# Attention's product with v in a piece for each block of tokens, at a rate of 0.75

## The chip, the core and the metric

The program runs on one core of one Trainium2 chip. A core has five engines that run side by side, each with its own instruction stream: TensorE (PE, with PEld for its weight loads), VectorE (DVE), ScalarE (ACT), GpSimd (POOL) and SyncE (SP, which here only issues DMA). Every engine takes its instructions in order; one that waits holds up all that stand behind it. The metric is the device time of one execution in microseconds (us), and lower is better.

## What is computed

Three stages follow one another, all in float32. Attention runs over 8 batches with 8 heads, 576 tokens and a head width of 64; keys and values are first averaged in groups of 8 tokens, so that each token looks at 72 of them.

```python
k_p = k.reshape(B, H, Sp, pool, D).mean(axis=3)
v_p = v.reshape(B, H, Sp, pool, D).mean(axis=3)
scores = scale * np.matmul(q, k_p.transpose(0, 1, 3, 2))
attn = softmax(scores)
x = np.matmul(attn, v_p)          # then as 4608 tokens x 512
h = (x @ w1) * (x @ w2) @ w3 @ w_out
r = np.maximum(h @ w_in, 0.0)
out = (r * r) @ w_out2
```

The inner widths are 1024 for w1, w2 and w3, and 2048 for the last stage.

## The kernel before

**Arithmetic.** A float32 operand is held as two parts, high and low, in a format that TensorE takes in one pass (fp32r); `mm3` makes each product of three matmuls (high by high, high by low, low by high). `split` writes such a pair: a copy on ACT for the high part, a subtraction on DVE for the low one.

**Stages.** `fold` first multiplies w3 by w_out into one matrix, W. Then come nine blocks of 512 tokens. Block i runs `stage_ab(i, u)` for u from 0 to 7 (a = x @ w1, b = x @ w2 for 128 of the 1024 columns, and gf = a * b on DVE), and two steps behind it `stage_w(i, u)`, which adds that piece times W into four accumulators. In the profile the matmuls of the blocks are `ps_w<-x,wt` (the first half of w1 and w2, held in SBUF), `ps_w<-x,un` (the second half, read back from DRAM through a ring of 8 buffers) and `acc<-gt,Wt`. After the last block comes the third stage (`ps_a` to `ps_d`, `ps_h`, `o`), which holds nothing of attention.

**Attention** makes x, and is spread through `fold` and the blocks. `build_tasks` writes one list of tasks: transposed keys (`pe_kt`), scores (`pe_s`), transposed probabilities (`pe_t`), and the product with v (`pe_av`, tile `ps_av`). A batch has two halves, of 256 and 320 tokens; `pe_av` is called for each of them with four pairs of heads (hp), and makes 128 of x's 512 rows, in one tile of PSUM from the pool of two that all attention tasks share. Three matmuls come from `mm3` and one holds the rest (`rem`). The result is copied into the x tiles of the blocks that the tokens fall in. Seven halves lie in two blocks: in batch 0 (256 tokens and 64), batch 1 (192 and 128), batch 2 (128 and 192), batch 3 (64 and 256), all in the second half, and in the first half of batch 5 (192 and 64), batch 6 (128 and 128) and batch 7 (64 and 192).

**What sets the order.** `run_mm` calls `tick` after each 6 matmuls. A tick runs the pumps: `attend`, which adds `rate[0]` to a credit and writes tasks from the head of the list while the credit is at least 1, and feeders that prepare the weights of the third stage (`feed_quarters`). A task has a list `need`; when it is not in `done`, the list stands still. The x tiles are a pool of 8, which is two blocks of four, so a task that writes block n must wait until `("ab", n - 2)` is done, that is until the `stage_ab` steps of block n - 2 are all written. For a half that lies in two blocks, `need` goes by the later one. Before block i, `until(lambda: tokens_ready((i + 1) * TB))` ticks with no matmul between until all the halves that block i needs have been written. It does so 2, 9, 5, 4, 5 and 4 times ahead of blocks 1, 2, 3, 5, 6 and 7, and not ahead of the others. A scheduler afterwards moves instructions within small bounds on each engine.

**DMA.** SP issues all loads in order. `load_v(b + 1)`, called after batch b's last `pe_av`, issues 24 and more; `load_q` 16 of queries, which DVE transposes (`qT<-qraw`). Raw weights (`raw`, `rq`) are loaded there too, and ACT takes each up first (L136).

Of the kernel before, what the change touches and what calls it, by code (L numbers as in the profile page):

```python
# [8 lines left out]
F32 = mybir.dt.float32  # L9
# [6 lines left out]
P = 128  # L16
TB = 512
# [12 lines left out]
def attn_moe_moe2_kernel(  # L30
# [16 lines left out]
    nc = tc.nc  # L47
# [16 lines left out]
    QT = []  # L64
# [43 lines left out]
    def f32(ap):  # L108
        return ap.bitcast(F32)
# [45 lines left out]
    def mm3(ps, pairs, first=True, last=True):  # L155

        todo = []
        for (ah, al), (bh, bl) in pairs:
            todo += [(ah, bh), (ah, bl), (al, bh)]
        n = len(todo)  # L160
        return [
            (lambda a=a, b=b, i=i: nc.tensor.matmul(  # L162
                ps, a, b, start=first and i == 0, stop=last and i == n - 1))
            for i, (a, b) in enumerate(todo)
        ]
# [63 lines left out]
    def xt_tile(blk, c):  # L229
        if (blk, c) not in xt:  # L230
            xt[blk, c] = x_p.tile([P, 2, TB], F32R, tag="x", name=f"x_{blk}_{c}")
        return xt[blk, c]
# [164 lines left out]
        dl = rem[RB:2 * RB, :, c0:c0 + n]  # L397
        nc.vector.tensor_sub(dl, ps[RB:2 * RB, :2, :n], f32(dl))

    def pe_av(b, hf, hp):  # L400
        hi, lo, rem = atts[b, hf]
        s0 = QT[HALF[hf][0]][0]
        w = sum(QT[i][1] for i in HALF[hf])
        ps = ps_at.tile([P, TB], F32, tag="at", name="ps_av")
        st = [vl[:, i, hp].rearrange("p a d -> p (a d)") for i in range(2)]
        for m in mm3(ps[:, :w], [(st, [t[:, hp, :w] for t in (hi, lo)])], last=False):
            m()
        nc.tensor.matmul(
            ps[:, :w], vr[:, hp].rearrange("p a d -> p (a d)"), rem[:, hp // 2, :w],
            start=False, stop=True)  # L410
        t0 = b * S + s0
        pieces = []
        o = 0
        while o < w:
            blk, c = divmod(t0 + o, TB)
            n = min(w - o, TB - c)
            pieces.append((blk, c, o, n))
            o += n

        for blk, c, o, n in pieces:  # L420
            nc.scalar.copy(xt_tile(blk, hp)[:, 0, c:c + n], ps[:, o:o + n])
        for blk, c, o, n in pieces:
            t = xt_tile(blk, hp)
            nc.vector.tensor_sub(t[:, 1, c:c + n], ps[:, o:o + n], f32(t[:, 0, c:c + n]))  # L424
        done.add(("av", b, hf, hp))

    NG = B * len(QT)

    def s_end(hf):
        return QT[HALF[hf][-1]][0] + QT[HALF[hf][-1]][1]  # L430

    def build_tasks():


        order = []
        pend = []

        def put(fn, need=()):
            order.append((need, fn))

        def put_pend(n=1):
            for _ in range(min(n, len(pend))):
                order.append(pend.pop(0))

        def kt(b):
            for part in range(2):
                put(lambda part=part: pe_kt(b, part))

        def sc(g):
            for half in range(2):  # L450
                put(lambda half=half: pe_s(g, half))
                put_pend()

        kt(0)
        sc(0)
        put(lambda: load_q(0, 1))
        for g in range(NG):
            b, i = divmod(g, len(QT))
            hf = 0 if i in HALF[0] else 1

            if i + 1 == HALF[1][0] and b + 1 < B:
                put(lambda b=b: load_q(b + 1, 0))
            if i + 1 == len(QT) and b + 1 < B:
                put(lambda b=b: load_q(b + 1, 1))
                kt(b + 1)
            if g + 1 < NG:
                sc(g + 1)
            if i == HALF[hf][0]:
                put_pend(len(pend))
            for part in range(2):  # L470
                put(lambda g=g, part=part: pe_t(g, part))
                put_pend()
            if i == HALF[hf][-1]:
                need = [("v", b)]

                last = (b * S + s_end(hf) - 1) // TB
                if last >= 2:
                    need.append(("ab", last - 2))
                for hp in range(NP):
                    def av(b=b, hf=hf, hp=hp):  # L480
                        pe_av(b, hf, hp)
                        if hf == 1 and hp == NP - 1 and b + 1 < B:
                            load_v(b + 1)
                    pend.append((need, av))
                if b < EARLY:
                    put_pend(len(pend))
        put_pend(len(pend))
        return order
# [17 lines left out]

    def tokens_ready(n):

        b, s = divmod(n, S)
        halves = [(bb, h) for bb in range(b) for h in range(2)]  # L510
        if s:
            halves.append((b, 0))
            if s > QT[HALF[1][0]][0]:
                halves.append((b, 1))
        return all(("av", bb, h, hp) in done for bb, h in halves for hp in range(NP))


    wt = {}
# [523 lines left out]
    setup_consts()  # L1042
    fold()
    until(lambda: tokens_ready(TB))
    rate[0] = 0.6
    fh1 = [(nm_, w, kc) for nm_, w in (("w1", w1), ("w2", w2)) for kc in range(KD)]
    feeds = []
    second = []
# [151 lines left out]
```

## Time and profile before

| | us |
|---|---|
| runs | 1644.57, 1641.16, 1642.05 |
| median | 1642.05 |
| profiled execution | 1644.58 |
| its span in the trace | 1642.8 |
| `fold`, from the start of the trace | 0 to 136 |
| block 0 | 136 to 240 |
| blocks 1 to 8 | 240 to 907 |
| third stage | 907 to 1643 |

The blocks begin at 135.9, 240.3, 325.2, 413.8, 502.3, 582.3, 666.3, 755.1 and 834.0 us. A time in a row is the start within the span; the number in brackets is what the engine stood idle before it, and whom it waited for. Records of matmuls overlap, so the spacing of starts tells what one costs. `PEclk` is the share of TensorE's full clock that was granted.

### The profile page before, as it was taken

To read this page: it belongs to the slowest core of one execution; us is meant where nothing else is said; L and a number is where in the kernel's file an instruction comes from. 1 tells how busy PE (TensorE), PEld (TensorE's weight loads), DVE (VectorE), ACT (ScalarE), POOL (GpSimd) and SP (SyncE) were. 2 spreads that over 40 slices of the span, in tenths; PEclk is the share of its full clock that TensorE was granted. 3 is DMA by queue.
4 is the path that set the end of the run, shared out by engine and by line. 5 is a ranking of instruction groups with operands and counts; after the bars stand their busy time and mean duration, and the time that the engine had idled before them with its cause. 6 is when DMAs were issued, how large, how long until landed. Compare 5 with 4: busy or idle time off the path is not lost.

```text
span 1642.8 us, 24999 instructions
## 1 busy us (share of the span) xinstructions
PE 1561.0 (95%) x8480; PEld 1309.5 (80%) x8480; DVE 1024.7 (62%) x1842; ACT 749.8 (46%) x1833; POOL 148.9 (9%) x194
## 2 busy tenths in 40 slices
PE   7899789999998999999999999999999999999998
PEld 5556567777777778777887788899899899899998
DVE  8898757565856457575626548547864776476432
ACT  4454425444443234445323566456444645454441
POOL 1132302111111011111101000000000000000000
PEclk9999799999999999999999999999999999999999
DMA  8454575747466554565726877677767777776764
GB/s 260 146 156 128 161 212 141 206 131 204 132 171 183 161 164 153 169 174 178 262 84 199 281 193 221 188 213 203 238 188 212 211 206 195 206 213 186 210 209 153
DMA packets 277854, 308.26 MB, mean 188 GB/s; under 512 B 98272, under 2 KB 163808, under 8 KB 277728
## 3 DMA queue, kind: packets, MB, share of 16 engines
q1 hardware_dynamic: 272544, 297.23, 61.6%
q10 hardware_dynamic: 5184, 9.44, 1.6%
q8 instruction: 68, 1.11, 0.3%
q14 instruction: 58, 0.48, 0.1%
HBM read 247.46 MB, written 56.62 MB: 185 GB/s over the span
## 4 chain that ended last, share of the span: by engine, by line
PE 66%; DVE 10%; DMA 7%; issue 3%; ACT 2%; SPq 2%; POOL 2%; DVEq 0%; POOLq 0%; ACTq 0%
PE o L964 17%; PE ps_w L162 16%; PE acc L162 7%; PE ps_a L876 5%; PE ps_c L876 5%; PE ps_d L876 5%; PE ps_h L162 3%; PE o L1020 3%; PE ps_b L876 2%; DMA rq<-in_moe_w_in_dram 2%; DVE x2o L114 1%; PE ps_s L343 1%; DMA raw<-in_moe_w_out_dram 1%; DMA un<-u_w 1%; SPq L276 1%
## 5 line engine op out<-in xcount | busy, mean ns | idle before, releaser
L964 PEld LDWEIGHTS o<-un,gt 128*128 128x128 f32 x2688 | 342.5, 191 | 19.3 <-DVE gt L114 7.3
L964 PE MATMUL o<-un,gt 128*128 128x256 f32 x2688 | 347.2, 283 | 6.1 <-DVE gt L114 5.7
L114 DVE TENSOR_TENSOR gt<-gs,gt 128x512 fp32r<-128x512 f32 x221 | 151.8, 690 | 198.7 <-ACT gt L113 198.4
L162 PE MATMUL ps_w<-x,wt 128*128 128x512 f32 x864 | 231.9, 411 | 9.5 <-DVE x L424 4.6
L162 PE MATMUL ps_w<-x,un 128*128 128x512 f32 x864 | 221.1, 403 | 11.0 <-DMA un<-u_w 9.4
L162 PE MATMUL acc<-gt,Wt 128*128 128x512 f32 x864 | 218.0, 396 | 4.2 <-ACT st L650 2.8
L113 ACT CAST gt<-gs 128x512 fp32r<-128x512 f32 x221 | 135.9, 616 | 158.5 <-PE o L964 128.0
L162 PEld LDWEIGHTS ps_w<-x,un 128*128 128x128 f32 x864 | 162.0, 192 | 46.4 <-DMA un<-u_w 11.5
L162 PEld LDWEIGHTS ps_w<-x,wt 128*128 128x128 f32 x864 | 161.4, 195 | 46.2 <-DVE x L424 7.0
L162 PEld LDWEIGHTS acc<-gt,Wt 128*128 128x128 f32 x864 | 158.8, 188 | 38.7 <-ACT st L650 3.8
L360 ACT ACTIVATE att<-ps_s,mx 128x72 f32<-128x72 f32 (+1 forms) x320 | 98.1, 320 | 103.8 <-DVE mx L358 97.7
L883 ACT ACTIVATE r<-r 128x512 f32<-128x512 f32 x96 | 60.6, 632 | 122.1 <-DVE r L913 121.7
L876 PE MATMUL ps_a<-x2o,un 128*128 128x512 f32 x384 | 99.6, 395 | 2.1 <-ACT p L901 2.1
L876 PE MATMUL ps_c<-x2o,un 128*128 128x512 f32 x384 | 99.5, 395 | 0.0
L876 PE MATMUL ps_d<-x2o,un 128*128 128x512 f32 x384 | 98.5, 391 | 0.0
L624 DVE TENSOR_TENSOR gf<-asb,ps_w 128x512 f32<-128x512 f32 x72 | 49.2, 684 | 71.0 <-PE ps_w L162 68.7
L884 ACT ACTIVATE gs<-r 128x512 f32<-128x512 f32 x137 | 85.4, 630 | 3.4 <-ACT gt L113 0.5
L876 PEld LDWEIGHTS ps_c<-x2o,un 128*128 128x128 f32 x384 | 70.6, 191 | 13.4 <-DVE u L907 0.3
L876 PEld LDWEIGHTS ps_a<-x2o,un 128*128 128x128 f32 x384 | 69.3, 190 | 14.7 <-ACT p L901 2.5
L876 PEld LDWEIGHTS ps_d<-x2o,un 128*128 128x128 f32 x384 | 69.8, 189 | 12.9
L620 ACT COPY asb<-ps_w 128x512 f32<-128x512 f32 x72 | 42.3, 588 | 81.2 <-PE ps_w L162 80.9
L113 ACT CAST gt<-gf 128x512 fp32r<-128x512 f32 x72 | 44.8, 623 | 74.2 <-DVE gf L624 65.6
(123 smaller groups left out, 2133.2 us busy)
## 6 DMA issues: line engine op xcount, KB each, us to landing
un<-u_w SPq DMA_DIRECT2D x144, 256.0 KB
un<-u_A SPq DMA_DIRECT2D x128, 256.0 KB
un<-u_S SPq DMA_DIRECT2D x128, 256.0 KB
un<-u_oA SPq DMA_DIRECT2D x128, 256.0 KB
un<-u_oS SPq DMA_DIRECT2D x128, 256.0 KB
raw<-in_moe_w_dram SPq DMA_DIRECT2D x32, 512.0 KB
raw<-in_moe_w_out_dram SPq DMA_DIRECT2D x24, 512.0 KB
x2d<-st ACTq DMA_DIRECT2D x36, 256.0 KB
```

Source lines behind the costliest of these rows:

```text
L113: nc.scalar.copy(hi, src)
L114: (eng or nc.vector).tensor_sub(lo, src, f32(hi))
L162: (lambda a=a, b=b, i=i: nc.tensor.matmul(ps, a, b, start=first and i == 0, stop=last and i == n - 1))
L276: nc.sync.dma_start(f32(vr)[r0:r0 + RM, c, 1, :], vhl[c * RM:(c + 1) * RM, i // 2, NP, :])
L360: nc.scalar.activation(av[:, h0 + h], sv[:, h], ACTF.Exp, bias=mx[:n, h:h + 1], scale=scale, accum_out=sm[:n, h0 + h:h0 + h + 1])
L620: nc.scalar.copy(asb, ps)
L624: nc.vector.tensor_mul(gf, asb, pss[1])
L876: nc.tensor.matmul(ps, l, r, start=first and j == 0, stop=j == len(todo) - 1, skip_group_check=True)
L883: nc.scalar.activation(t, src, ACTF.Relu)
L884: nc.scalar.activation(take(name), t, ACTF.Square)
L964: nc.tensor.matmul(ps, l, r, start=u == 0 and m != 5 and o % 2 == 0 and j == 0, stop=u == NU - 1 and j == 2, skip_group_check=True)
L1020: nc.tensor.matmul(acc[o][:, y * PC:(y + 1) * PC], l, r, start=u == 0 and y == 0 and j == 0, stop=u == U2 - 1 and j == 2, skip_group_check ...
```

## The change

`pe_av` makes the product for one piece only, the part of a half that falls in one block. `av_pieces` lists the pieces. In `build_tasks` each piece is a task of its own for each hp, and its `need` names its own block; `tokens_ready` asks for the pieces that lie before token n, and no longer for whole halves. The rate goes from 0.6 to 0.75. `split` writes the two parts, as the two loops did.

```diff
-    def pe_av(b, hf, hp):
+    def av_pieces(b, hf):
         s0 = QT[HALF[hf][0]][0]
         w = sum(QT[i][1] for i in HALF[hf])
-        for m in mm3(ps[:, :w], [(st, [t[:, hp, :w] for t in (hi, lo)])], last=False):
...
+    def pe_av(b, hf, hp, piece):
+        hi, lo, rem = atts[b, hf]
+        blk, c, o, n = piece
+        for m in mm3(ps[:, :n], [(st, [t[:, hp, o:o + n] for t in (hi, lo)])], last=False):
+            m()
+        nc.tensor.matmul(
+            ps[:, :n], vr[:, hp].rearrange("p a d -> p (a d)"), rem[:, hp // 2, o:o + n],
+            start=False, stop=True)
+        t = xt_tile(blk, hp)
+        split(t[:, 0, c:c + n], t[:, 1, c:c + n], ps[:, :n])
+        done.add(("av", b, hf, hp, blk))
...
-                last = (b * S + s_end(hf) - 1) // TB
-                if last >= 2:
-                    need.append(("ab", last - 2))
+                for piece in pieces:
+                    need = [("v", b)]
+                    if piece[0] >= 2:
+                        need.append(("ab", piece[0] - 2))
...
-    rate[0] = 0.6
+    rate[0] = 0.75
```

The list grows from 255 tasks to 283, by 28 `pe_av` calls. They bring 112 matmuls and 112 weight loads; ACT and DVE keep their number of instructions for x. The ticks without matmuls ahead of the blocks are gone, at all nine. `load_v(1)`, which stood just ahead of block 0, now stands within it. `feed_quarters` is some seven steps further back in its list at the ends of the middle blocks.

How TensorE's instructions stand at the start of block 6. The block's first matmuls are `ps_w...<-x_0_...,wt`; a number behind a name tells tiles of one name apart, and `x_0` to `x_3` are the four tiles of a block. Before:

```order
L162 MATMUL acc_5812<-gt,Wt 128x512 x3
L162 MATMUL ps_av<-aT_6107,vl 128x256
L162 MATMUL ps_av<-aT_6108,vl 128x256
L162 MATMUL ps_av<-aT_6107,vl 128x256
L408 MATMUL ps_av<-aR,vr 128x256
L343 MATMUL ps_s<-kbd,qT 128x144 x2
L162 MATMUL ps_w_6415<-x_0_5488,wt 128x512
```

And now:

```order
L162 MATMUL ps_av<-aT_6124,vl 128x128
L162 MATMUL ps_av<-aT_6125,vl 128x128
L162 MATMUL ps_av<-aT_6124,vl 128x128
L420 MATMUL ps_av<-aR,vr 128x128
L162 MATMUL ps_w_6425<-x_0_4872,un 128x512 x3
L162 MATMUL ps_w_6425<-x_1_4896,un 128x512 x3
L162 MATMUL ps_w_6425<-x_2_4910,un 128x512 x3
L162 MATMUL ps_w_6425<-x_3_4927,un 128x512 x3
L162 MATMUL acc_5907<-gt,Wt 128x512 x3
L162 MATMUL acc_5908<-gt,Wt 128x512 x3
L162 MATMUL acc_5909<-gt,Wt 128x512 x3
L162 MATMUL acc_5910<-gt,Wt 128x512 x3
```

Here the last of the four products that block 6 needs (it completes x_3) is followed by 24 matmuls of block 5, and then by block 6's first, `ps_w_6467<-x_0_5591,wt`; before, the product that completes x_0 stood two small matmuls ahead of its reader.

VectorE at the same place. Before:

```order
L331 STREAM_TRANSPOSE qT<-qraw 128x256
L114 TENSOR_TENSOR gt<-gf,gt 128x512
L424 TENSOR_TENSOR x_0_5488<-ps_av,x_0_5488 128x128
L424 TENSOR_TENSOR x_0_6358<-ps_av,x_0_6358 128x128
L357 TENSOR_REDUCE mx<-ps_s 128x4
```

And now:

```order
L331 STREAM_TRANSPOSE qT<-qraw 128x256
L114 TENSOR_TENSOR x_0_5591<-ps_av,x_0_5591 128x128
L619 TENSOR_TENSOR gf<-asb,ps_w_6315 128x512
L357 TENSOR_REDUCE mx<-ps_s 128x4
L358 TENSOR_SCALAR mx<-mx 128x4
L114 TENSOR_TENSOR gt<-gf,gt 128x512
```

The subtraction that completes x_0 still stands behind a transpose of queries; block 7's part of it (x_0_6358 before) is no longer beside it.

TensorE in block 0, where it reads the second halves of w1 and w2 for the first time (`un`). Before:

```order
L162 MATMUL ps_w_1761<-x_1_741,un 128x512 x3
L162 MATMUL ps_av<-aT_1703,vl 128x320
L162 MATMUL ps_av<-aT_1704,vl 128x320
L162 MATMUL ps_av<-aT_1703,vl 128x320
L408 MATMUL ps_av<-aR,vr 128x320
L162 MATMUL ps_av<-aT_1703,vl 128x320
L162 MATMUL ps_av<-aT_1704,vl 128x320
L162 MATMUL ps_av<-aT_1703,vl 128x320
L408 MATMUL ps_av<-aR,vr 128x320
L162 MATMUL ps_w_1761<-x_2_782,un 128x512 x3
```

And now:

```order
L420 MATMUL ps_av<-aR,vr 128x192
L162 MATMUL ps_av<-aT_1723,vl 128x128
L162 MATMUL ps_av<-aT_1724,vl 128x128
L162 MATMUL ps_av<-aT_1723,vl 128x128
L420 MATMUL ps_av<-aR,vr 128x128
L162 MATMUL ps_av<-aT_1723,vl 128x128
L162 MATMUL ps_av<-aT_1724,vl 128x128
L162 MATMUL ps_av<-aT_1723,vl 128x128
L420 MATMUL ps_av<-aR,vr 128x128
L162 MATMUL ps_w_1781<-x_2_782,un 128x512 x3
```

Ahead of the product of x_2 there now stand, counted back to the middle of the unit before, four products with v of 192 columns and two of 128, where there were two of 320.

## Rows read from the trace of the kernel before

**Rows 1.** The page: busy us, share of the span and instructions of each engine.

```profile
PE 1561.0 (95%) x8480; PEld 1309.5 (80%) x8480; DVE 1024.7 (62%) x1842; ACT 749.8 (46%) x1833; POOL 148.9 (9%) x194
```

**Rows 2.** Windows of block 0 and of blocks 1 to 8: length, busy us of each engine, PEclk, DMA share, GB/s.

```profile
136.00:240.00 104.00, 86.62 (x388) 68.57 (x387) 70.49 (x142) 43.34 (x146) 25.61 (x26) 0.90 0.58 164
240.00:907.00 667.00, 637.05 (x2954) 509.92 (x2954) 401.16 (x803) 273.81 (x873) 95.52 (x126) 0.98 0.57 171
```

**Rows 3.** Groups by line: count, busy us, mean ns, idle before and its enders.

```profile
L162 PE MATMUL ps_w<-x,wt 128*128 128x512 f32 x864 | 231.9, 411 | 9.5 <-DVE x L424 4.6 <-ACT x L421 2.5 <-DVE gf L624 2.2
```

**Rows 4.** Timeline of PE at the starts of blocks 2, 3, 5, 6, 7: start, us, [idle before].

```profile
333.99 1.20 PE L162 MATMUL ps_w<-x,wt 128*128 128x512 f32 x4 [0.31 <-DVE x L424]
...
417.73 0.50 PE L162 MATMUL ps_w<-x,wt 128*128 128x512 f32 x1 [0.53 <-DVE x L424]
...
585.01 0.74 PE L162 MATMUL ps_w<-x,wt 128*128 128x512 f32 x2 [1.01 <-DVE x L424]
586.58 0.59 PE L162 MATMUL ps_av<-aT,vl 128*128 128x256 f32 x3 [0.84 <-DVE x L424]
...
669.74 0.80 PE L162 MATMUL ps_w<-x,wt 128*128 128x512 f32 x1 [2.76 <-DVE x L424]
...
763.78 1.72 PE L162 MATMUL ps_w<-x,wt 128*128 128x512 f32 x4 [2.52 <-ACT x L421]
```

**Rows 5.** Timeline of DVE at the start of block 6.

```profile
668.47 0.45 DVE L331 STREAM_TRANSPOSE qT<-qraw 128x256 f32<-128x256 f32 x1 [5.00 <-DMA qraw<-in_q_dram]
668.83 0.65 DVE L114 TENSOR_TENSOR gt<-gf,gt 128x512 fp32r<-128x512 f32 x1
669.40 0.48 DVE L424 TENSOR_TENSOR x<-ps_av,x 128x128 fp32r<-128x128 f32 x2
```

**Rows 6.** Timeline of ACT at the start of block 7.

```profile
762.98 0.65 ACT L136 ACTIVATE raw<-raw 128x512 f32<-128x512 f32 x1 [3.72 <-DMA raw<-in_moe_w_out_dram]
763.53 0.41 ACT L421 CAST x<-ps_av 128x64 fp32r<-128x64 f32 x2
```

**Rows 7.** Windows at three block starts and within a block, columns as in rows 2.

```profile
582.00:592.00 10.00, 8.04 (x33) 5.78 (x33) 7.56 (x18) 4.39 (x12) 2.54 (x2) 0.83 0.55 166
666.00:676.00 10.00, 7.24 (x33) 5.73 (x32) 4.35 (x16) 2.88 (x16) 1.15 (x1) 0.83 0.66 166
716.00:756.00 40.00, 40.00 (x199) 33.51 (x197) 23.74 (x48) 17.00 (x62) 3.87 (x6) 1.00 0.55 163
760.00:770.00 10.00, 7.48 (x28) 5.12 (x28) 5.96 (x12) 3.64 (x9) 1.73 (x3) 0.83 0.44 170
```

**Rows 8.** Timeline of PE where products with v of 256 and 320 columns follow closely.

```profile
754.20 0.51 PE L162 MATMUL ps_av<-aT,vl 128*128 128x256 f32 x3
754.55 0.28 PE L408 MATMUL ps_av<-aR,vr 96*128 96x256 f32 x1
...
628.02 0.60 PE L162 MATMUL ps_av<-aT,vl 128*128 128x320 f32 x3
628.46 0.31 PE L408 MATMUL ps_av<-aR,vr 96*128 96x320 f32 x1
```

**Rows 9.** Timeline of PE in `fold`: matmuls of 128 columns, plain float32.

```profile
109.37 1.72 PE L548 MATMUL ps_w<-ident,v 128*128 128x128 f32 x14
110.93 0.60 PE L390 MATMUL ps_t<-ident,att 128*128 128x128 f32 x4
```

**Rows 10.** Groups of weight loads, of 128 columns and of 64, columns as in rows 3.

```profile
L343 PEld LDWEIGHTS ps_s<-kbd,qT 128*128 128x128 f32 x256 | 40.2, 198 | 13.6 <-DVE aT L114 2.7 <-issue 2.5 <-ACT att L360 2.2
...
L343 PEld LDWEIGHTS ps_s<-kbd,qT 128*64 128x64 f32 x64 | 6.9, 136 | 6.0 <-issue 2.4 <-DVE aR L398 1.3 <-DVE aT L114 0.9
```

**Rows 11.** Timeline of PE in block 0, where its last wait for `un` ends.

```profile
212.33 2.08 PE L162 MATMUL ps_w<-x,un 128*128 128x512 f32 x4 [3.58 <-DMA un<-u_w]
```

**Rows 12.** Timeline of PE within blocks 3 and 4: waits on attention's own results.

```profile
437.83 0.76 PE L343 MATMUL ps_s<-kbd,qT 128*128 128x144 f32 x4 [2.31 <-DVE aT L114]
...
531.75 0.63 PE L395 MATMUL ps_t<-ident,rem 128*96 128x128 f32 x2 [4.15 <-ACT att L360]
```

More of the change, by code (lines that the diff above doesn't have):

```diff
@@ L398, in pe_t @@
         nc.vector.tensor_sub(dl, ps[RB:2 * RB, :2, :n], f32(dl))
-    def pe_av(b, hf, hp):
-        hi, lo, rem = atts[b, hf]
+    def av_pieces(b, hf):
         s0 = QT[HALF[hf][0]][0]
         w = sum(QT[i][1] for i in HALF[hf])
-        ps = ps_at.tile([P, TB], F32, tag="at", name="ps_av")
-        st = [vl[:, i, hp].rearrange("p a d -> p (a d)") for i in range(2)]
-        for m in mm3(ps[:, :w], [(st, [t[:, hp, :w] for t in (hi, lo)])], last=False):
[L407 to L411, printed above, removed]
         pieces = []
@@ L414, in pe_av @@
         while o < w:
-            blk, c = divmod(t0 + o, TB)
+            blk, c = divmod(b * S + s0 + o, TB)
             n = min(w - o, TB - c)
@@ L418, in pe_av @@
             o += n
[L420 to L425, printed above, removed]
+        return pieces
+    def pe_av(b, hf, hp, piece):
+        hi, lo, rem = atts[b, hf]
+        blk, c, o, n = piece
+        ps = ps_at.tile([P, TB], F32, tag="at", name="ps_av")
+        st = [vl[:, i, hp].rearrange("p a d -> p (a d)") for i in range(2)]
+        for m in mm3(ps[:, :n], [(st, [t[:, hp, o:o + n] for t in (hi, lo)])], last=False):
[6 more added lines that the diff above has]
+        done.add(("av", b, hf, hp, blk))
     NG = B * len(QT)
-    def s_end(hf):
-        return QT[HALF[hf][-1]][0] + QT[HALF[hf][-1]][1]
     def build_tasks():
@@ L473, in build_tasks, with av @@
             if i == HALF[hf][-1]:
-                need = [("v", b)]
-                last = (b * S + s_end(hf) - 1) // TB
-                if last >= 2:
-                    need.append(("ab", last - 2))
[L479 to L484, printed above, removed]
+                pieces = av_pieces(b, hf)
+                for piece in pieces:
+                    need = [("v", b)]
+                    if piece[0] >= 2:
+                        need.append(("ab", piece[0] - 2))
+                    for hp in range(NP):
+                        def av(b=b, hf=hf, hp=hp, piece=piece, end=piece is pieces[-1]):
+                            pe_av(b, hf, hp, piece)
+                            if hf == 1 and hp == NP - 1 and end and b + 1 < B:
+                                load_v(b + 1)
+                        pend.append((need, av))
                 if b < EARLY:
@@ L507, in tokens_ready @@
     def tokens_ready(n):
[L509 to L515, printed above, removed]
+        return all(
+            ("av", b, hf, hp, piece[0]) in done
+            for b in range(B) for hf in range(2) for piece in av_pieces(b, hf)
+            if piece[0] * TB + piece[1] < n for hp in range(NP))
     wt = {}
```

## Prediction, made before the changed kernel was run

> **What bounds the kernel now.** I read the page first: TensorE is busy for 95% of the span [rows 1]. The stage windows come next, since the change touches block 0 and blocks 1 to 8 alone. Block 0 is 104 us long and holds 86.62 us of TensorE's work; blocks 1 to 8 are 667 us long and hold 637.05 [rows 2]. So TensorE sets the pace in the blocks, and what can be won there without taking work away is 30.0 us of idle time in blocks 1 to 8, 17.4 us in block 0, and what a lowered clock adds. Every matmul that is added costs its full spacing, unless it lies in an idle stretch.
>
> The groups by line say how much of the idle time hangs on x: the first matmuls of a block, `ps_w<-x,wt`, stood idle 9.5 us in all, 4.6 of it until a DVE subtraction into x ended and 2.5 until an ACT copy into x did [rows 3]. The timeline gives the places: the starts of blocks 2, 3, 5, 6 and 7, with 0.31, 0.53, 1.01 + 0.84, 2.76 and 2.52 us, together 8.0 us [rows 4]. They fit the lists of the code: the half that block i needs may be written only when all `stage_ab` steps of block i - 1 are, so its product with v, its copy and its subtraction stand a few matmuls ahead of their reader. Whatever holds DVE or ACT for some microseconds there goes on to TensorE. At block 6 it is a transpose for which DVE stood idle 5.00 us until queries had landed; the subtraction into x is behind it [rows 5]. At block 7 it is ACT's first step on a raw weight, with 3.72 us of waiting for the load; the copy into x is behind that [rows 6].
>
> The clock has a part as well. In the 10 us around the starts of blocks 5, 6 and 7 the granted share is 0.83, while 40 us inside block 6 run at 1.00 [rows 7]. TensorE had just been idle there, and part of each window was granted the lower level, 1.2 GHz. At 10 x (1 - 0.83) this is 1.7 us for each of three starts, 5.1 us.
>
> **The change, part by part.** *The boundaries.* Each piece of block i now waits only for block i - 2, so it may be written anywhere within block i - 1. In the program as it is ordered now, the last product that fills a tile of x stands, by my count of the matmuls between, at least 3.9 us of TensorE's work ahead of that tile's first reader (block 3; 8 us or more at the other starts where tokens were waited for), against some 0.5 to 1.4 us before at most of them. DVE and ACT still meet their loads in the same order: the subtraction into x_0 of block 6 still follows a transpose of queries. But 3.9 us and more of cover is over the 2.76 us that was the largest wait [rows 4]. I take all of it: -8.0 us of waits and -5.1 us of clock, **-13.1 us**. What is late next at such a place is `gf` and `gt`, for which `stage_w` stands two steps behind.
>
> *The shorter matmuls.* Outside `fold`, six halves (batches 1, 2, 3, 5, 6, 7) were one product for each of four hp, 4 matmuls each, 16 in a half. They become pieces: four of 192 columns, four of 128, three of 64, and one of 256. The old ones start 0.44 us apart by three at 320 columns, 145 ns each, and 0.35 us by three at 256, 117 to 120 ns [rows 8]. Removed: 16 x (3 x 145 + 3 x 120) = 12.7 us. Added: 16 x 120 = 1.9 us for the one of 256, and 11 x 16 = 176 matmuls below 256 columns. Those have no row: no fp32r matmul under 256 columns runs before. Three bounds:
> - By columns alone. From 120 ns at 256 and 145 at 320 the slope is 0.4 ns a column, so 94, 69 and 43 ns at 192, 128 and 64. Sum 64 x 94 + 64 x 69 + 48 x 43 = 12.5 us; net 12.5 + 1.9 - 12.7 = +1.7.
> - By the weight load that each one has. Loads of 128 columns take 198 ns and of 64 columns 136 [rows 10]: 62 ns for 64 columns, about 124 for 128, if the rest overlaps. And plain float32 matmuls of 128 columns start 1.56 us apart by 14, 111 ns each [rows 9]. At 112 ns: 19.7 us; net **+8.9**.
> - By the price of float32. Such a matmul is two records in the trace (the scores' line is called 160 times, and [rows 10] count 256 + 64 loads for it), so one of 128 columns costs 2 x 111 ns, 1.73 ns a column. If a short fp32r matmul runs like that: 333, 222 and 111 ns, 64 x 333 + 64 x 222 + 48 x 111 = 40.8 us; net +30.0.
>
> I take the middle one: the loads in [rows 10] have the same 128 columns as those of v, and at 111 ns [rows 9] matmuls and loads of that size keep step. Against a gain of 14.1 us in the other terms the break-even lies at (14.1 + 12.7 - 1.9) / 176 = 141 ns for a short matmul.
>
> By a rule of the Trainium skill ("TensorE: Matmul & The Clock Gate", "LDWEIGHTS (loading the stationary operand)") a load takes its columns divided by 1.2 ns, and columns of the weights alone count. That is an estimate of 107 ns for 128, so a piece of 64 columns would cost as much as one of 128; it speaks against cutting, and by it this term would be +8.0 rather than +8.9. The same page ("Back-to-back issue gap") gives about 81 ns at 128 columns, which would make it +3.5 with that for all 176; the 111 ns of [rows 9] agrees with the former, not with this.
>
> *Block 0.* Its two pieces of batch 0 are within `fold` and the block's start, where TensorE is idle 17.4 of 104 us [rows 2]; I set their cost at nothing, cover gone 16 x 112 ns = 1.8 us. More attention now stands ahead of the last wait for `un`, of 3.58 us [rows 11]: four products of 192 columns and two of 128 (24 matmuls by 112 ns, 2.7 us) for two of 320 (8 by 145 ns, 1.2 us). They fill 1.5 us of the wait, if the load lands when it did. But `load_v(1)` now issues its DMAs within this block on SP, and raw weights are taken in another order there. Bounds: the whole wait goes (-3.6), or `un` comes as late as a raw load kept ACT waiting (+3.7) [rows 6]. I take **-1.0**.
>
> *The rate.* 0.75 for 283 tasks is like 0.676 for the 255 of before, some 13% denser. Total work is the same. Denser tasks can make TensorE meet results of attention that are not ready: such waits are there (2.31 and 4.15 us) [rows 12]. I set it at nothing, since the scheduler has spread the tasks and the empty ticks, which bunched them at six starts, are gone. `feed_quarters` lags by seven steps; they are done before the third stage needs them. ACT and DVE issue the same number of instructions for x.
>
> Sum: -13.1 + 8.9 - 1.0 = **-5.2 us**. On the profiled execution, 1644.58 (span 1642.8), this gives 1639.4; the median of the runs is 2.5 lower, so I forecast 1642.05 - 5.2 = 1636.9, **1637 us**.
>
> **The rivals.**
> - *Short fp32r matmuls at float32's price* (the slower side). Place: the 176 matmuls under 256 columns. -13.1 + 30.0 - 1.0 = +15.9, **1658 us**. It decides above 141 ns a matmul. For it: nothing in the trace shows this format short, and the nearest short matmuls are float32's. Against it: for 256 to 320 columns the price is by columns.
> - *They go by their columns.* -13.1 + 1.7 - 1.0 = -12.4, **1630 us**. For it: [rows 8] fall on a line. Against it: loads of 128 columns.
> - *The waits move rather than go.* DVE and ACT still wait for `qraw` and `raw` in order, and a `gt` or a score behind them stops TensorE instead. At half the gain: -6.5 + 8.9 - 1.0 = +1.4, **1643 us**. For it: the 5.00 us of [rows 5] is over the smallest cover of 3.9. Against it: the other starts have 8 us or more.
> - *Denser attention meets its own results more often*, with two tiles of PSUM for all of it. Waits within blocks 1 to 8 are 30.0 - 8.0 = 22 us; half as many again is +11: -5.2 + 11 = +5.8, **1648 us**. For it: [rows 12]. Against it: the rate rises by an eighth only.
>
> **How the numbers follow.** Forecast 0.36, float32's price 0.27, by columns 0.12, waits that move 0.15, denser attention 0.10. A measurement of this kernel can tell about 0.2%, 3.3 us, from no change. Faster takes the third case and most of the first (0.30): 0.42. Within 0.2% are the fourth, most of it, and the rest of the first: 0.19. Slower is the second, nearly all, and most of the fifth and a little of the fourth: 0.39. Both signs hold much, so the forecast's own range stands apart: 1631 to 1645 (boundaries from -13.1 to -8, block 0 between -3.6 and +3.7, the short matmuls around 95 to 124 ns). The whole range, from the third case, with a little more won in block 0, to the second: 1627 to 1659.
>
> **What would show it.** The row of `ps_w<-x,wt` should lose its waits on x (7.1 of 9.5 us), and the windows at the three starts should read 0.95 or more. The spacing of `ps_av` records at 192, 128 and 64 columns decides between the first three cases at once: 112 ns alike, 94 to 43, or 333 to 111. Idle time in 240 to 907 us below 22 us would refute denser waits. I am wrong if a short piece takes more than 141 ns, or if DVE's wait for queries still reaches x.

## The result, and the profile after

The changed kernel takes 1654.06 us (median of 6 runs, 1650.22 to 1657.58) against 1642.33 us; the ratio is 1.0068, with a 95% interval from 1.0055 to 1.0081. It is slower by 11.7 us, where the forecast was faster by 5.2. The first trace is of the fastest of the six runs (span 1648.4); a later one of the same program has a span of 1653.5, nearer to the median, and both are used.

The page of the changed kernel, first trace. Busy time of TensorE, and the group that [rows 3] showed:

```profile
PE 1560.8 (95%) x8592; PEld 1314.8 (80%) x8592; DVE 1023.8 (62%) x1842; ACT 750.3 (46%) x1833; POOL 148.7 (9%) x194
...
L162 PE MATMUL ps_w<-x,wt 128*128 128x512 f32 x864 | 228.2, 405 | 1.8 <-DVE gf L619 0.6
```

The waits on x are gone from blocks 1 to 8, as the change meant: 9.5 us of idle time before this group are now 1.8, of which 0.4 us, in block 0, are a wait for x. But TensorE's idle time from 240 to 907 us has not fallen from 30.0 to the 22 of the forecast; it is 667.00 - 633.04 = 34.0 us (first trace, columns as in [rows 2]):

```profile
240.00:907.00 667.00, 633.04 (x3019) 512.68 (x3018) 387.23 (x777) 269.88 (x864) 91.89 (x124) 0.98 0.55 163
```

What took the place of the waits on x is in the view of TensorE's waits, 240 to 907 us, first of the kernel before (who waited, for whom, us in total, times, longest):

```profile
PE ps_w L162 <- DVE x L424: 4.6, 4, 2.8
PE ps_t L395 <- ACT att L360: 4.2, 1, 4.2
...
PE ps_w L162 <- ACT x L421: 2.5, 1, 2.5
...
PE ps_av L162 <- DVE x L424: 1.3, 2, 0.8
```

and then of the changed kernel:

```profile
PE ps_av L162 <- DVE x L114: 16.4, 5, 6.3
PE ps_t L390 <- DVE vhl L254: 3.8, 1, 3.8
PE acc L162 <- ACT st L645: 3.3, 2, 2.9
```

7.1 us of waiting for x by its readers have become 15.1 us more of waiting by `ps_av` itself. A product with v waits for a subtraction into x when it wants a PSUM tile: the pool has two, and a tile is free when the product before the last has been copied and subtracted. The second trace, at the start of block 7, first TensorE, then ACT, then DVE:

```profile
763.21 1.53 PE L162 MATMUL ps_w<-x,wt 128*128 128x512 f32 x6
764.58 0.47 PE L162 MATMUL ps_av<-aT,vl 128*128 128x192 f32 x3
764.89 0.27 PE L420 MATMUL ps_av<-aR,vr 96*128 96x192 f32 x1
765.00 0.50 PE L162 MATMUL ps_av<-aT,vl 128*128 128x192 f32 x3
765.33 0.27 PE L420 MATMUL ps_av<-aR,vr 96*128 96x192 f32 x1
771.72 0.95 PE L162 MATMUL ps_av<-aT,vl 128*128 128x192 f32 x3 [6.11 <-DVE x L114]
```

```profile
769.26 0.62 ACT L113 CAST oq<-sq 128x512 fp32r<-128x512 f32 x1 [3.15 <-DMA u_oA<-oq]
769.79 0.53 ACT L113 CAST x<-ps_av 128x192 fp32r<-128x192 f32 x2
```

```profile
769.91 0.69 DVE L114 TENSOR_TENSOR oq<-sq,oq 128x512 fp32r<-128x512 f32 x1 [3.07 <-ACT oq L113]
770.64 0.76 DVE L137 TENSOR_SCALAR wq<-raw 128x512 uint32<-128x512 uint32 x2
771.32 0.35 DVE L114 TENSOR_TENSOR x<-ps_av,x 128x192 fp32r<-128x192 f32 x1
```

Block 7 has begun without a wait. Three products for block 8 then come close together; the third finds both tiles full. The copies that would empty them stand on ACT behind `oq`, a step of the third stage's weight preparation, which stood idle 3.15 us for a store; the subtraction stands on DVE behind more steps of it, on `oq` and `wq`. It is the same order of things as in [rows 5] and [rows 6], with PSUM in x's place.

The clock. Windows of 10 us at the starts of blocks 5, 6, 7, of the first trace (columns as in [rows 2]), and then of blocks 6 and 7 in the second, set so that each holds the whole of its stretch at the lower clock, as those of [rows 7] do:

```profile
582.00:592.00 10.00, 9.37 (x53) 7.58 (x52) 4.09 (x9) 3.95 (x10) 0.20 (x1) 1.00 0.92 247
671.00:681.00 10.00, 6.45 (x27) 5.53 (x28) 6.29 (x14) 3.76 (x9) 1.07 (x1) 0.66 0.86 287
763.00:773.00 10.00, 6.30 (x26) 5.38 (x27) 6.89 (x14) 3.10 (x8) 3.16 (x2) 0.66 0.68 213
```

```profile
676.00:686.00 10.00, 6.47 (x27) 5.55 (x28) 6.28 (x14) 3.74 (x9) 1.06 (x1) 0.66 0.86 285
768.00:778.00 10.00, 6.28 (x26) 5.34 (x27) 6.87 (x14) 3.07 (x8) 3.15 (x2) 0.66 0.65 205
```

Against 0.83 at all three in [rows 7]: block 5's start is cured, blocks 6 and 7 are worse. Lost are 6.8 us in either trace (0.34 + 0.34 of 10 us), where 5.1 were lost before. Over 240 to 907 us the share is 0.98 in the first trace, as it was [rows 2].

The short matmuls. Two sets of 128 columns between long ones, first trace:

```profile
658.94 0.44 PE L162 MATMUL ps_av<-aT,vl 128*128 128x128 f32 x3
659.23 0.27 PE L420 MATMUL ps_av<-aR,vr 96*128 96x128 f32 x1
659.34 1.59 PE L162 MATMUL ps_w<-x,un 128*128 128x512 f32 x6
660.77 0.44 PE L162 MATMUL ps_av<-aT,vl 128*128 128x128 f32 x3
661.05 0.27 PE L420 MATMUL ps_av<-aR,vr 96*128 96x128 f32 x1
```

Four start within 0.40 us. Over all sets at the full clock the median of four is 0.361 us at 64 columns, 0.394 at 128 and 0.425 at 192: the spacing within a set is 112 ns, and the first is cheaper, since its weights were loaded under the long matmul ahead (in the trace that load starts at 658.71 us, with the last long matmul). By these, and 0.478 and 0.583 for sets of 256 and 320, the term is 16 x 0.425 + 16 x 0.394 + 12 x 0.361 + 4 x 0.478 - 12 x (0.478 + 0.583) = +6.6 us.

### The profile page after: what moved, and what is told of

It is laid out like the page before. It is cut to its first block, busy times and chain, and to the rows that moved or that the text cites. A ratio compares the mean times of both kernels' runs of the same rounds, so it can differ in the third digit from the quotient of the medians.

```text
span 1648.4 us, 25179 instructions
## 1 busy us (share of the span) xinstructions
PE 1560.8 (95%) x8592; PEld 1314.8 (80%) x8592; DVE 1023.8 (62%) x1842; ACT 750.3 (46%) x1833; POOL 148.7 (9%) x194
## 4 chain that ended last, share of the span: by engine, by line
PE 52%; DVE 6%; DMA 3%; issue 2%; SPq 1%; POOL 1%; ACT 1%; POOLq 0%; DVEq 0%; ACTq 0%
PE o L959 18%; PE ps_w L162 8%; PE ps_c L871 5%; PE ps_a L871 4%; PE ps_d L871 4%; PE acc L162 4%; PE ps_h L162 3%; PE o L1015 3%; PE ps_b L871 2%; DVE x2o L114 1%; POOL wq L671 1%; DMA u_oA<-oq 1%; DMA raw<-in_moe_w_out_dram 1%; DVE x2r L842 1%; SPq L276 1%
## 5 line engine op out<-in xcount | busy, mean ns | idle before, releaser
L162 PE MATMUL ps_w<-x,wt 128*128 128x512 f32 x864 | 228.2, 405 | 1.8 <-DVE gf L619 0.6
L162 PE MATMUL ps_w<-x,un 128*128 128x512 f32 x864 | 217.5, 400 | 7.2 <-DMA un<-u_w 6.2
L871 PEld LDWEIGHTS ps_c<-x2o,un 128*128 128x128 f32 x384 | 69.6, 189 | 15.1 <-DVE u L902 2.4
L871 PEld LDWEIGHTS ps_d<-x2o,un 128*128 128x128 f32 x384 | 69.7, 189 | 13.4 <-DVE r L908 0.6
```

Of the source, the lines that this page charges most:

```text
L162: (lambda a=a, b=b, i=i: nc.tensor.matmul(ps, a, b, start=first and i == 0, stop=last and i == n - 1))
L871: nc.tensor.matmul(ps, l, r, start=first and j == 0, stop=j == len(todo) - 1, skip_group_check=True)
```

## The experiments

In many of them the whole time hides where it went, so the stretch from the start of block 1 to the start of block 8 is read as well: 593.7 us before, 599.9 and 601.1 in the two traces of the changed kernel.

**The three parts, one by one.** Cutting alone, with the condition of the later block:

```diff
-                    if piece[0] >= 2:
-                        need.append(("ab", piece[0] - 2))
+                    if pieces[-1][0] >= 2:
+                        need.append(("ab", pieces[-1][0] - 2))
...
-    rate[0] = 0.75
+    rate[0] = 0.66
```

> The product with v is cut into pieces, but each piece still waits for the later of its half's two blocks, and the rate is 0.66, which for 283 tasks is the pace that 0.6 was for 255. So this is the cutting alone. Three theories of the 11.7 us that the changed kernel lost against my sum of -5.2. Bunching: cutting costs what its matmuls cost (176 of 112 ns and the 16 of batch 0, +9.6 us of TensorE's work against before), and the rest is lost where own conditions and the higher rate put three products with v in one tick: 1652. Cutting: each piece takes one of two PSUM tiles, so more turns of these tiles cost beyond the matmuls, at any rate: 1657 or more. Rate: the cutting is as cheap as in the sum, and only the denser list costs: 1651 to 1652 as well, told apart by the next two.

1659.8 us against 1641.8, ratio 1.0098 (1.0077 to 1.0120): +18.0 us. That is what the cutting theory said, and 8 us beyond both others. Then the changed kernel with `rate[0] = 0.66`, so cut and with its own condition:

> The changed kernel at the rate 0.66, the pace of before. There are empty ticks again ahead of blocks 1, 2, 3, 6 and 7 (3, 9, 7, 2, 6), so part of the waits at the block starts comes back. Bunching: one tick with three products instead of four, so below the changed kernel in spite of that, 1645 to 1650. Cutting: no better than the changed kernel, 1654 or more. Rate: 1645 to 1648.

1659.0 us, ratio 1.0096 (1.0077 to 1.0115). The own condition is worth 0.8 us, which these intervals cannot tell from nothing; cutting theory again. And the kernel before with `rate[0] = 0.75`:

> The kernel before with the rate 0.75 and nothing else. Seven ticks hold two or more products with v, where three did, and 2 or 3 empty ticks stay ahead of blocks 1, 2, 3, 5, 6, 7. Rate: this alone loses, 1650 or more. Bunching: some of it, 1644 to 1649, as the products come together but are fewer. Cutting: no change, 1641 to 1643.

1642.8 us, ratio 1.0007 (0.9994 to 1.0020): no change, and the rate theory falls. So the change reads as a sum of steps: cutting +18.0, own condition -0.8, rate from 0.66 to 0.75 with a list that is 28 tasks longer -4.9, together about +12.

**Are the products too close together?** In `attend`, `min(credit[0], 3.0)` became `min(credit[0], 1.0)` in the changed kernel.

> The changed kernel with one number else: while the list stands still, the credit is held at 1 and no longer at 3, so that no tick holds more than one product with v (four ticks held three, one more held two). Bunching: the waits of products with v for a tile of PSUM (some 14 us of idle time and at the starts of blocks 4, 6 and 7 waits of 2.5, 5.2 and 6.3 us) fall by about half: 1646 to 1650. Cutting and rate: no change, 1653 to 1655.

1652.9 us, ratio 1.0061 (1.0041 to 1.0081), within the spread of the changed kernel. My theory that ticks with three products make the loss falls. With one product in a tick the waits for PSUM were fewer, 4.9 us where they were 16.4, and others took their place; the stretch is 600.6 us, as long as before this edit:

```profile
PE ps_av L162 <- DVE x L114: 4.9, 3, 2.7
```

So the 16.4 us are not the loss by themselves: with two thirds of them gone the time stays.

**What does cutting cost by itself?** The kernel before, where `pe_av` issues its four matmuls once for each piece, into the same tile; task, condition and rate as before:

```diff
+        for blk, c, o, n in pieces:
+            for m in mm3(ps[:, o:o + n], [(st, [t[:, hp, o:o + n] for t in (hi, lo)])], last=False):
+                m()
+            nc.tensor.matmul(
+                ps[:, o:o + n], vr[:, hp].rearrange("p a d -> p (a d)"),
+                rem[:, hp // 2, o:o + n], start=False, stop=True)
```

> The kernel before, where a product with v that lies in two blocks is issued as two sets of four matmuls, one for the columns of each block, into the same PSUM tile and in the same task, with the rate 0.6 and the old condition. So 112 matmuls and weight loads more, and nothing else moved. Matmul price as in my sum (112 ns for a short one, +9.6 us with batch 0): 1650 to 1652. If a part of them is hidden where TensorE waits anyway: 1645 to 1649. If a cut costs more than its matmuls even so: 1655 or more, as the 18 us of the run with all cut and the old condition.

1672.0 us, ratio 1.0188 (1.0169 to 1.0207), +29.5. This is the third case, with some 11 us more than the 18 that it named, and more than the changed kernel itself. The stretch, windows of 15 us at the starts of its blocks 5, 6 and 7, and its waits on x from the start of block 1 to that of block 8:

```profile
243.83:860.78 616.95, 581.04 (x2715) 471.57 (x2715) 360.69 (x739) 247.13 (x830) 92.97 (x123) 0.96 0.56 167
592.50:607.50 15.00, 13.74 (x56) 12.05 (x57) 5.67 (x18) 5.51 (x21) 2.12 (x3) 0.66 0.48 134
684.00:699.00 15.00, 14.56 (x58) 12.62 (x58) 4.95 (x17) 4.63 (x19) 1.62 (x3) 0.66 0.94 318
780.00:795.00 15.00, 14.41 (x57) 12.34 (x57) 13.15 (x32) 7.50 (x24) 3.16 (x4) 0.66 0.63 211
```

```profile
PE ps_w L162 <- DVE x L424: 7.0, 5, 3.4
PE ps_w L162 <- ACT x L421: 6.0, 2, 3.0
```

The clock is 0.66 over 15 us at all three, 15.3 us lost where 5.1 were, and the waits on x have grown from 7.1 to 13.0 us. Of the 23.2 us by which the stretch is longer, the clock over all of it (0.96 where it was 0.98) makes some 13, and TensorE's idle time (35.9 us where it was 28.6) 7; some 3 us are left for the added matmuls. At 1.2 GHz a set of four short matmuls took 0.71 us at the least, and 0.76 to 0.95 at the median by width, about double. The four products of a half stand right at the start of the block there, 32 short matmuls beside the wait on x. In the changed kernel a part of them stands inside the block before.

The same with a PSUM tile for each piece:

> As the run with cut matmuls only, but each piece takes a PSUM tile of its own out of the pool of two, still in one task. Turns of the tiles: 28 more turns, each of which waits for copy and subtraction of the turn before the last, make it 4 to 8 us slower than the run with cut matmuls only. No such price: within 2 us of it, and then the 8 us beyond the matmuls, that the run with the old condition showed, come from the longer list of tasks and its order.

1670.1 us, ratio 1.0176 (1.0157 to 1.0194). 28 more turns of the two tiles cost nothing that can be seen. So the reason that the cutting theory gave, the turns, falls, and only its time was right.

The same cut put where no block starts: products within one block are issued as 128 columns and the rest, those across two blocks stay whole.

```diff
+        inner = [(o, n) for _, _, o, n in pieces] if len(pieces) == 1 else [(0, w)]
+        if len(pieces) == 1 and b:
+            inner = [(0, P), (P, w - P)]
```

> The kernel before, where the products with v that lie in one block (eight halves of batches 1 to 7) are issued in two sets of matmuls, 128 columns and 128 or 192, into one tile; the ones that lie in two blocks stay whole. 128 matmuls more, inside the blocks and not at their starts. At 112 ns each: 64 x (224 - 120) + 64 x (224 - 145) ns = 11.7 us. If short matmuls lower the clock only where TensorE also waits, as at the block starts (12.9 us of clock in the run with cut matmuls only): 1652 to 1656. If they lower it wherever they stand in a row: 1660 to 1675.

1665.3 us, ratio 1.0142 (1.0127 to 1.0157), +23.5. The time is that of the second expectation: cutting costs inside the blocks as well. But its cause is not the clock, which is 0.98 in both stretches. TensorE was busy 8.3 us longer, which goes with the added matmuls, and idle 7.5 us longer (the trace is of a run of 1661.7 us). The two windows, the kernel before first:

```profile
240.25:833.98 593.73, 565.18 (x2640) 450.89 (x2638) 364.86 (x742) 249.56 (x832) 91.28 (x123) 0.98 0.59 174
```

```profile
242.79:852.34 609.55, 573.49 (x2747) 460.48 (x2746) 363.61 (x741) 247.99 (x832) 92.36 (x123) 0.98 0.57 169
```

**The own condition without the cutting.** The product stays whole and waits for the earlier block; the later block's part goes through DRAM:

```diff
+            if x and blk >= 2:
+                split(r[:, 0], r[:, 1], ps[:, o:o + n])
+                nc.sync.dma_start(d, f32(r))
...
+    def put_late(b, hf, hp):
+        nc.sync.dma_start(f32(t)[:, :, c:c + n], r[hp])
```

> The product with v is whole again, and waits only for the earlier of the two blocks; the later block's part is split into two SBUF tiles, stored to DRAM, and loaded into the x tile when that is free (24 stores and 24 loads more on SP, no matmul more). So this is the own condition without the cutting, at the rate 0.6; empty ticks are left ahead of blocks 1, 2 and 3 (2, 8, 6). If the waits at the block starts are won as in my sum, for blocks 5, 6 and 7 at least: 6.5 of 8.0 us and 5.1 us of clock, so 1629 to 1634. If they move to other places, as the difference of the two conditions with cut products (0.8 us) says: 1640 to 1644.

> The same at the rate 0.66, with one empty tick in all. Gains at all starts as in my sum: 1628 to 1632. Waits that move: 1640 to 1645, as with 0.6.

1651.1 us (ratio 1.0064, 1.0045 to 1.0083) and 1659.1 us (1.0104, 1.0084 to 1.0124). Neither expectation had it slower. In the first one's trace the clock in block 1 to 8 is up (0.99) and the waits on x are small, but TensorE is idle 38.6 us in the stretch instead of 28.6; the 48 more DMAs on SP are part of this run, so it doesn't price the condition alone. It gives no sign of the 13 us of my sum.

**The changed kernel once more.**

> The changed kernel itself once more, for a second trace: the first one is of its fastest run (1650.2 where the median is 1654.1). 1652 to 1656. If the waits of products with v for a PSUM tile at the starts of blocks 4, 6 and 7 (2.5, 5.2, 6.3 us) belong to the program and not to one run, they are there again within a microsecond or two, and the clock at 1.2 GHz behind them.

1654.1 us, ratio 1.0076 (1.0052 to 1.0100), and waits of 4.9 and 6.1 us at blocks 6 and 7 again: they belong to the program. Block 0 is 108.5 us long here and 105.5 in the first trace (104.3 before); the last wait for `un` is 5.35 and 4.82 us instead of 3.58 [rows 11]. The other waits for `un` are smaller: all of them in block 0 are 6.2 us in the first trace and 6.3 here, where they were 9.4. What took it back are waits on attention's own results and on PSUM that the kernel before did not have there, or had at 0.6 us (the second and third line, first trace). TensorE's idle time in block 0 is some 18 us in both traces where it was 17.4; the longer block 0 of the second trace goes with a clock of 0.87 instead of 0.90:

```profile
217.55 0.80 PE L162 MATMUL ps_w<-x,un 128*128 128x512 f32 x1 [5.35 <-DMA un<-u_w]
PE ps_t L390 <- ACT att L360: 6.4, 2, 3.8
PE ps_av L162 <- DVE x L114: 2.6, 2, 1.5
```

**Weight preparation taken out of the blocks.** `feed_quarters` waits until the third stage, in both kernels:

```diff
-        if not fh1 and quarters and not operands and ticks[0] % rate_q[0] == 0:
+        if second and quarters and not operands and ticks[0] % rate_q[0] == 0:
```

> The kernel before with the feeder of the third stage's weights held back until the third stage, so that no weight preparation of that stage runs on ACT, DVE, POOL and SP in blocks 0 to 7. The time of the whole is then another (the preparation falls into the third stage, and the time is read for the blocks alone): what counts is the stretch from the start of block 1 to the start of block 8, 593.7 us before. If preparation ahead of copies and subtractions makes the waits: 575 to 585. If not: 590 or more.

> The same done to the changed kernel; the stretch was 599.9 us there, 6.2 longer than before. If the gain at the block starts is lost because the emptying of the PSUM tiles stands behind weight preparation, the difference to the run without preparation of the kernel before turns round: the 9.5 us of matmuls less 8.0 of waits and some clock, so 0 to 4 us shorter. If attention's own chain loses it: 5 us longer or more, as with preparation.

The whole times are 1748.7 and 1767.8 us, since the third stage waits for its weights. The stretches, before and changed:

```profile
238.04:789.86 551.82, 547.84 (x2640) 445.75 (x2638) 271.44 (x565) 212.59 (x766) 57.79 (x101) 1.00 0.43 121
```

```profile
241.47:806.73 565.26, 558.19 (x2723) 455.79 (x2721) 265.54 (x558) 211.19 (x764) 57.14 (x101) 0.99 0.41 116
```

And the kernel before's waits in it, all that the view lists:

```profile
PE acc L162 <- ACT st L650: 1.8, 1, 1.8
PE ps_av L162 <- DVE aR L398: 0.9, 1, 0.9
PE ps_av L162 <- DVE x L424: 0.8, 1, 0.8
PE ps_t L390 <- issue: 0.2, 1, 0.2
```

This is the run that shows what my 13 us hung on. With the old condition, the empty ticks and the late products all in place, but without weight preparation (its steps on ACT, DVE and POOL, its DMAs and their traffic, all at once), no reader of x waits at all: the stretch is 41.9 us shorter, TensorE is idle 4.0 us in it instead of 28.6, and the clock is 1.00. The difference of the two kernels did not turn round as I expected; it grew, from 6.2 (7.3 in the second trace) to 13.4 us. Without the waits, the change has nothing to win and only pays: TensorE is busy 10.4 us longer, matmuls and some clock, and idle 3.1 us longer. If the two add up, the change wins some 6 to 7 us in this stretch with preparation, and costs 13.

**Which part of the preparation?** Three tries. The feeder pauses in a block's last and first step and goes faster otherwise (changed kernel):

> The changed kernel, where the feeder of the third stage's weights pauses in the last and the first step of a block, and takes a step each third tick in place of each fourth otherwise. If weight preparation at the block starts holds up the emptying of PSUM tiles: the waits of 5.2 and 6.3 us at blocks 6 and 7 shrink to under 2 us each, and the time is 1642 to 1649. If the preparation holds up other things wherever it stands, or is not the cause: 1652 to 1657.

1701.5 us, but my edit left the pause on after the last block, and the third stage had to wait for its weights, so only the stretch counts: 606.4 us against 601.1, with 4.3 us of waiting for PSUM still at block 7. It didn't help. Raw loads five steps earlier, in both kernels:

```diff
+    quarters = sets[0][:1]
+    for x, s in enumerate(sets):
+        quarters += s[1:3] + (sets[x + 1][:1] if x + 1 < len(sets) else []) + s[3:]
```

> The kernel before, where the raw weights of each next unit of the third stage are loaded five steps of the feeder earlier, right behind the step that frees their buffers; nothing else is moved. If the waits on x at the block starts come from weight preparation that waits for its loads in front of the copies into x on ACT (3.72 us at block 7), rather than from the condition on whole halves, then a part of the 8.0 us of these waits goes without any change in attention: 1632 to 1639. If the condition is the cause, or the loads are late for want of bandwidth: 1641 to 1645.

> The same in the changed kernel. If the emptying of the PSUM tiles waits behind preparation that waits for its loads: the waits of 3.1, 4.9 and 6.2 us at blocks 4, 6 and 7 shrink to half or less, 1643 to 1649. If preparation is held up by its stores (ACT waited 3.14 us for one at block 7) or attention's own chain is the cause: 1652 to 1656.

1645.1 us (ratio 1.0019, 1.0009 to 1.0029) and 1657.5 (1.0103, 1.0087 to 1.0119): 3 us slower each. The waits did go in part. In the kernel before, those on x are 4.9 us instead of 7.1, and the stretch is 590.0 us; that of block 7 stays (first line). In the changed kernel those for PSUM are 10.8 us instead of 16.4 (second line), and only block 7's is over 1.4 us:

```profile
PE ps_w L162 <- ACT x L421: 3.2, 1, 3.2
PE ps_av L162 <- DVE x L114: 10.8, 5, 6.4
```

So late loads have a part in it at some starts, but not at block 7, and the whole program wins nothing. Stores of the third stage's weights issued by POOL, in both:

```diff
-        nc.sync.dma_start(unit(key)[:, par], f32(t)[:, :, off:off + P])
+        (nc.sync if key[0] in ("w1", "w2") else nc.gpsimd).dma_start(unit(key)[:, par], f32(t)[:, :, off:off + P])
...
-            nc.sync.dma_start(out_unit(unit(("o" + name, u))), f32(t)[:, :, off:off + PC])
+            nc.gpsimd.dma_start(out_unit(unit(("o" + name, u))), f32(t)[:, :, off:off + PC])
```

> The changed kernel, where the stores of the third stage's prepared weights are issued by POOL and no longer by SP, where they stand behind raw loads (SP needed 8.05 us for two of them ahead of block 7). At block 7, ACT waited 3.14 us for such a store before it could go on to the copies into x, and TensorE then 6.28 us for a PSUM tile. If the stores on SP hold up the emptying of the PSUM tiles: the waits of 4.9 and 6.2 us at blocks 6 and 7 go to under 2 us each, 1642 to 1650. If it is the preparation's work on ACT and DVE as such: 1652 to 1657. What POOL's issue costs is not known from any run; it stands in front of POOL's own additions of the preparation, and could make it slower.

> The same in the kernel before. If the stores on SP hold up ACT and DVE, the waits on x of 2.8 and 2.5 us at blocks 6 and 7 go in part: 1633 to 1639. If not: 1641 to 1645.

1681.4 us (1.0242, 1.0224 to 1.0259) and 1657.0 (1.0085, 1.0071 to 1.0100). The wait at block 7 is gone in the changed kernel, but those at blocks 4 and 6 stay (4.1 and 5.7 us), and POOL pays for 192 stores:

```profile
L186 POOL DMA_DIRECT2D u_S<-oq x64 | 46.4, 728 | 0.0
```

At 728 ns and more each, 139 us of POOL's time in all, ahead of attention's own steps on POOL. The runs don't settle which part of the preparation holds up the copies.

**Short matmuls without the preparation's waits.**

> The run with cut matmuls only, with the third stage's weight preparation held back until that stage (the whole time is another, and the stretch from the start of block 1 to the start of block 8 is read: 593.7 us in the kernel before and 617.0 with cut matmuls; 551.8 in the kernel before without preparation). If short matmuls lower the clock only beside a wait that something else makes: the cut costs its matmuls, 558 to 562 us, and the granted clock stays at 1.00. If short matmuls lower the clock by themselves: some 12 us more, 570 to 575.

The stretch is 582.5 us against 551.8 uncut, 30.7 more: above both expectations. TensorE is busy 18.9 us longer, which holds the matmuls and some clock, and idle 11.8 us longer:

```profile
240.60:823.09 582.49, 566.74 (x2736) 462.51 (x2735) 270.10 (x566) 213.43 (x767) 57.95 (x101) 0.99 0.40 115
```

So what cutting costs beyond its matmuls needs no wait that preparation makes. It does not lie everywhere either. Five of the seven blocks are 8.9 us longer together; block 1 is 11.4 and block 6 10.4 us longer, and these two hold waits and the lower clock:

```profile
240.60:334.90 94.30, 85.38 (x405) 68.94 (x405) 51.56 (x103) 33.95 (x132) 9.95 (x19) 0.96 0.48 133
656.12:747.35 91.23, 86.32 (x413) 69.86 (x412) 53.13 (x112) 38.96 (x138) 14.44 (x19) 0.96 0.57 173
```

Uncut, the two took 82.9 and 80.9 us, with 3.7 and 0.2 us idle instead of 8.9 and 4.9, and a clock of 1.00. The longest of these waits is of the kind in [rows 5]: DVE waits for queries, with steps of the block behind them:

```profile
274.41 0.45 DVE L331 STREAM_TRANSPOSE qT<-qraw 128x256 f32<-128x256 f32 x1 [4.54 <-DMA qraw<-in_q_dram]
276.76 1.65 PE L162 MATMUL acc<-gt,Wt 128*128 128x512 f32 x3 [4.01 <-ACT st L650]
```

Why cutting brings TensorE to such places at a worse moment stays open. One thing was not held still in any of the cut kernels: the scheduler moves instructions on the other engines too when matmuls are cut. About 18% of DVE's rows stand elsewhere in the kernel with cut matmuls only, and 7% between the two kernels without preparation. The kernel before with earlier raw loads has 20% moved, and lost 3 us, so moving alone need not cost 20; but it was not separated.

## Why the prediction was wrong

- **The waits on x** (-8.0): the step that failed. The waits did go, 7.1 us of them. I read them as made by the condition, with DVE and ACT as carriers. The run without preparation shows that the condition alone makes none: they come with preparation, whose steps and loads stand in front of attention's copies in the rows. That it is the order on ACT and DVE, and not the traffic, is read from rows and was not separated. [rows 5] and [rows 6] named the queries and the raw weight ahead of the copies; I counted the new cover (3.9 us and more) against x's reader, and did not ask who else waits for the same copies. The two PSUM tiles do, and the products for the next block reach them a little later in the same place: 15 us. Idle time in blocks 1 to 8 came to 34.0 us, not 22. That these waits alone make the loss is not shown: the run with one product in a tick has 4.9 us of them and the same time. A third tile was not tried. Neither sign of being wrong that I named came true (a short piece over 141 ns, queries that still reach x).
- **The clock** (-5.1): followed the waits. Block 5's start was cured, blocks 6 and 7 lost more; 6.8 us where there were 5.1, so nothing was won.
- **The short matmuls** (+8.9): right in kind and near in size, +6.6. The middle bound held, 112 ns alike at 64, 128 and 192 columns within a set; the price of float32 and the price by columns are both refuted. The time came out near the first of these rivals (1658 us) for another reason. By the rule of the Trainium skill ("TensorE: Matmul & The Clock Gate", "LDWEIGHTS (loading the stationary operand)") a weight load of 128 columns is estimated at 107 ns; the 112 ns here are near it.
- **That cutting costs its matmuls only**: the second step that failed, and the dearer one. The runs show +18 for cutting at the old pace and condition, +23 within blocks, +30 at their starts, for 6.6 us of matmuls in the first and third and a nominal 11.7 in the second. At the starts most of it is the clock (15.3 against 5.1 us at three starts) and longer waits on x; within blocks it is idle time and matmuls at an unchanged clock. Why a cut brings these waits is open.
- **Block 0** (-1.0): it became 1.2 and 4.2 us longer. The waits for `un` did shrink, by 3.2 us, which is near the better bound; that attention would wait for its own results (6.4 us) and for PSUM (2.6) within this block I had put at nothing.
- **The rate** (nothing): right for the kernel before (+0.9, within its interval). With the longer list it is worth some 4.9 us by the medians, though the two intervals just overlap.
- Of the rivals, *waits that move* had the mechanism, with half of the gain left over; *denser attention meets its own results* had the two tiles of PSUM, but blamed the rate, which is innocent.

No version here beats the kernel before.

## What to carry to other kernels

A wait that ends with a copy on an engine taken in order belongs to what stands ahead of the copy. Before you relax the condition of the one who waits, list everyone who waits for that same copy, PSUM tiles included, and take the suspected cause out altogether for one run: the stretch without it says how much there is to win. And a matmul cut in two is not priced by its own spacing alone; cut it in place, with nothing else changed, before counting on the rest of an edit.

## What was not expected of the hardware

Short fp32r matmuls of 64, 128 and 192 columns, each with a weight load of 128 columns, all start 112 ns apart, and the first one after a matmul of 512 columns is followed after some 30, 58 and 88 ns in the first trace. Where TensorE had just waited some 3 us and then ran short matmuls, the granted share over 15 us was 0.66, and a set of four took 0.71 to 0.95 us instead of 0.36 to 0.43. DMA issues on POOL took 725 to 913 ns in the mean of each kind.
